# Queries of batch 2 loaded earlier and transposed by the DMA crossbar, with the units round its memory sums in a new order

## The chip, the cores and the metric

The kernel runs on one core of a Trainium2 chip. Five engines work side by side, each through its own list of instructions in order: TensorE (PE, with its weight loads as PEld) multiplies, VectorE (DVE) and ScalarE (ACT) work elementwise and read TensorE's results out of PSUM, GpSimd (POOL) works elementwise on SBUF, and SyncE (SP) only issues transfers. POOL, SP and ACT issue transfers to 16 DMA engines that they share. An instruction that must wait holds everything behind it on its engine. The metric is the device time of one execution in microseconds (us).

## The reference

There are 8 batches of 8 heads, 576 tokens and 64 dimensions, and 32 memory slots a head. Tokens are pooled into the slots by softmax weights; each query attends to its head's 32 pooled slots; the result, 4608 tokens of 512 features, goes through a gated feed-forward block with 1536 inner features.

```python
a = np.exp(phi - phi.max(2)); a = a / a.sum(2)     # per head: 576 x 32
k_m, v_m = a.T @ k, a.T @ v                        # memory sums: 32 x 64
scores = (q @ k_m.T) / 8                           # 576 x 32
x = softmax(scores) @ v_m                          # heads side by side: 4608 x 512
out = (silu(x @ w_gate) * (x @ w_val)) @ w_out     # 512 -> 1536 -> 512
```

## The kernel before

Matrix products take bf16 inputs. A batch goes through these steps.

- *Loads.* POOL issues most of them: `load_k`, `load_v` and `load_q` (L97 to L110) convert float32 to bf16 on the way. Weights come in three blocks of 512 inner features: gate and value (`load_w`), then w_out (`load_wo`, which fills `WO`). POOL's loads land in the order of their issue. The program is written so that an issue waits for the landing of the eighth load before it, as the same completion counter is used again.
- *Memory sums.* `phi_exp` (L170) takes exponentials on ACT. `kv_items` (L292) returns two units: `run_sums` multiplies phi with k and v on TensorE (L230) and then, on VectorE, takes the reciprocal of the denominators (L262) and scales the sums (`kv_norm`, L268, recorded as L266); `kv_T` (L278) transposes the scaled sums on TensorE (L288) and copies them to SBUF as `kT` (L289).
- *Queries.* They are needed transposed, as `qT`. Batches 0 to 2 use `q_T` (L377): TensorE transposes 18 blocks of 128x128 against the identity, six to a PSUM bank, and VectorE or ACT copies each bank out (L337, L339). Batches 3 to 7 use `load_qT` (L114): SP issues one transfer that transposes through the DMA crossbar, SBUF to SBUF, once the queries have landed.
- *Scores and softmax.* `scores` (L392) multiplies `kT` with `qT` on TensorE and ACT takes the exponential.
- *Gated block.* The value sums are multiplied into the gate and value weights (`u_round`, giving U); then gate and value products, silu on ACT and the product with the values on VectorE give `h`.
- *Output.* w_out is applied by a fast multiplication with seven products for eight. `weight_sums(c)` builds four sums of w_out's block c on VectorE, the matrices `T`; POOL or VectorE builds the same kind of sums of `h`, called `S`. `products(b, ...)` (L689) returns for a batch its seven products of six units each in a flat list; a unit is two matmuls, 0.109 us each by the profile's chain. Units 0 to 5 gather in bank "s", 6 to 11 in bank "a", 12 to 17 in "c", 18 to 23 in "s" again; units 4 and 5 of a product use w_out's block 2, units 2 and 3 block 1. After a product, `keep` (L748) copies a bank out on ACT (p1, q6, p5) or `add` (L757) adds banks on VectorE into an output tile, which SP stores.

The order of all this is written out by hand: the program runs with a manual schedule, so each engine's list is the order of the calls. Two stages matter here.

The opening issues the loads of batches 0 and 1, then (L905 to L916) the gate and value weights, w_out block 0, k of batch 2, w_out block 1, phi of batch 2, w_out block 2, v of batch 2. Further loads are hung on steps of the gated block by `beside_sums` (L672): when the first block of batch 0 is done, phi of batch 3 and the queries of batch 2; later queries, k and v of batch 3.

After the gated block of batches 0 and 1 the loop starts with batch 2 (L997 to L1022). Its lists are `zero` and `one`, the output units of batches 0 and 1, `kv`, the two units of the memory sums of batch 2, and `q2`, the three units of its query transposes, all copied out by ACT. TensorE runs units 0 to 5 of `zero`, 6 to 11 of `zero`, 0 to 5 of `one`, the sums, two query units, eight units of `zero` that read T and S of blocks 0 and 1, `kv_T`, the last query unit, four units of `zero` that read T of block 2, and then the scores of batch 2. VectorE builds T of blocks 0 and 1, scales the sums, builds the first half of T of block 2, copies `kT`, and builds the second half; POOL waits for that half (`wait_for`, L645) before it builds two blocks of S for batch 1.

Of the kernel before, what the change touches and what calls it, by code (L numbers as in the profile page):

```python
# [14 lines left out]
def kernel(  # L15
# [19 lines left out]
    nc = tc.nc  # L35
# [39 lines left out]
    def bank(shape, dtype, name):  # L75
        tag = free.pop(0)
        t = ps.tile(shape, dtype, tag=tag, name=name)
        held[id(t)] = tag, t
        return t

    def done(*tiles):

        for t in tiles:
            free.append(held.pop(id(t))[0])
# [3 lines left out]
    def head_pairs(x):  # L88

        return x.rearrange("h s d -> (h s d)").rearrange("(i p f) -> p i f", i=NP, p=128)  # L90

    def load_phi(b, eng):
        t = inp.tile([128, NP, JK * M], FP32, tag="phi", name="t_phi")
        eng.dma_start(out=t, in_=head_pairs(phi[b]))
        phis[b] = t
# [9 lines left out]
    def load_q(b):  # L105

        t = inp.tile([128, NS * 128], BF16, tag=f"q{Q_SLOT[b]}", bufs=1, name="t_q")
        nc.gpsimd.dma_start(  # L108
            out=t,
            in_=q[b].rearrange("h s d -> (h s d)").rearrange("(p f) -> p f", p=128),  # L110
        )
        qs[b] = t

    def load_qT(b):  # L114

        qTs[b] = att.tile([128, NS, 128], BF16, tag="qT", name="t_qT")
        nc.sync.dma_start_transpose(out=qTs[b], in_=qs[b])
# [10 lines left out]
    def load_w(which, c, half=None):  # L128

        src = (moe_w_gate, moe_w_val)[which]  # L130
        split = half is not None
        if not half:
            W[which, c] = wpool.tile(
                [128, 2, NP, HC] if split else [128, NP, CH], BF16,
                tag=f"W{which}{c}", name=f"W{which}{c}",
            )
        f0, n = (half * HC, HC) if split else (0, CH)
        nc.gpsimd.dma_start(  # L138
            out=W[which, c][:, half] if split else W[which, c],
            in_=src[:, c * CH + f0:c * CH + f0 + n].rearrange("(i p) f -> p i f", p=128),  # L140
        )
# [9 lines left out]
    def load_wo(c):  # L151
        t = wpool.tile([128, 4, DM], BF16, tag=f"WO{c}", name=f"WO{c}")
        nc.gpsimd.dma_start(
            out=t,
            in_=moe_w_out[c * CH:(c + 1) * CH, :].rearrange("(i p) f -> p i f", p=128),
        )
        for i in range(4):
            WO[4 * c + i] = t[:, i]
        WOc[c] = t
# [8 lines left out]
    ephis, rSs, bkvs, kTs, es, atts = {}, {}, {}, {}, {}, {}  # L168
# [91 lines left out]
    def kv_reciprocal(b, p):  # L260
        r = att.tile([128, NG], FP32, tag="rS", name="t_rS")
        nc.vector.reciprocal(out=r, in_=p)  # L262
        rSs[b] = r
# [14 lines left out]
    def kv_T(b):  # L278


        kTs[b] = att.tile([128, 3, 128], BF16, tag="kT", name="t_kT")
        t = bkvs.pop(b)
        if b > 3:
            nc.sync.dma_start_transpose(out=kTs[b], in_=t.rearrange("p n x -> p (n x)"))
            return
        p = bank([128, 3, 128], BF16, "p_T")
        for n in (2, 0, 1):
            nc.tensor.transpose(p[:, n], t[:, n], ident)  # L288
        nc.vector.tensor_copy(out=kTs[b], in_=p)  # L289
        done(p)  # L290

    def kv_items(b, beside=None):  # L292


        def run_sums():
            o = 2 * D
            behind = b in esums
            own = beside and not behind
            if own:
                d = bank([128, NG], FP32, "p_S")  # L300
                kv_denominators(b, d)
                kv_reciprocal(b, d)
                done(d)
            p = [bank([128, CH], FP32, f"p_kv{g}") for g in range(NG)]
            if not (own or behind):
                kv_denominators(b, p[0][:, o:o + NG])
            kv_sum(b, p, (0, 1))
            if behind:
                beside()
                kv_denominators(b, p[0][:, o:o + NG])  # L310
            if not own:
                kv_reciprocal(b, p[0][:, o:o + NG])
            kv_norm(b, p)
            if beside and not behind:
                beside()

        return [run_sums, lambda: kv_T(b)]
# [17 lines left out]
    def copy(eng, out, in_):  # L335
        if eng == "a":
            nc.scalar.copy(out=out, in_=in_)  # L337
        else:
            nc.vector.tensor_copy(out=out, in_=in_)  # L339
# [307 lines left out]
    def quad_sums(qd):  # L647
# [22 lines left out]
                    subtract(nc.gpsimd, t[:, 2], A12, t[:, 1])  # L670

    beside_sums = {  # L672
        (0, 0): lambda: (load_phi(3, nc.gpsimd), load_q(2)),
        (1, 0): lambda: load_q(3),
        (0, 1): lambda: (load_k(3), load_v(3)),
    }
# [152 lines left out]
    def q_items(b, evac):  # L829
        return [lambda n=n: q_T(b, n, evac[n]) for n in range(3)]  # L830
# [14 lines left out]
    def u_values(b):  # L845

        u_round(b, (((1,), 1, (0, 1)),), "aa")
    def run(items):
        for x in items:
            x()  # L850
# [13 lines left out]
    def gv_slots(b):  # L864
        return [lambda s=s: gv_slot(b, s) for s in range(2 * NJF)]
# [42 lines left out]
    for c in range(1, NCH):  # L908
        for which in range(2):
            load_w(which, c)  # L910
    load_wo(0)
    load_k(2)
    load_wo(1)
# [35 lines left out]
    warm(8)  # L949


    g0, g1 = gv_slots(0), gv_slots(1)
    nc.scalar.preload_act_table_set("silu_and_others")
    run([u_half(0, (0,), 0, 0, "va")])
# [41 lines left out]
    for b in range(2, B):  # L996
        last = b + 1 == B  # L997
        exp_tables()
        if b == 2:
            load_qT(3)  # L1000
            phi_exp(2)
            (zero, ops0), (one, ops1) = products(0, ("c11",)), products(1, ("p1", "c11"))
            kv, q2 = kv_items(2), q_items(2, "aaa")
            run(zero[:6])
            sums = {n: f for n, f in zip(((1, 1), (0, 2), (1, 2)), late)}
            late.clear()
            sums[0, 2]()
            weight_sums(0)
            weight_sums(1)
            run(zero[6:12] + one[:6] + kv[:1] + q2[:2])  # L1010
            weight_sums(2, (0, 1))
            run(zero[12:16] + zero[18:22] + kv[1:] + q2[2:] + zero[16:18] + zero[22:24])
            weight_sums(2, (2, 3))
            ops0["c11"]()
            ops1["p1"]()
            wait_for(Ts[2][0:1, 3, 0, 0:1])
            for part in ((0, 1), (3,), (2,)):
                for c in (1, 2):
                    sums[1, c](part)
            loads(4)  # L1020
            backlog = one[6:12] + zero[36:] + one[12:36]
            ops = ops1  # L1022
        else:
            run(take(6))
        for g in range(NG):
            scores(b, g)
        if b > 2:
            ops["p1"]()
            u_values(b)
        else:  # L1030
            run(zero[24:36] + take(6))
        run(take(6))
        z_inv_v(b, 0)
        ops["c11"]()
        run(take(6))
        if not last:
            phi_exp(b + 1)
        z_inv_v(b, 1)
        if b > 2:
            norm(b, 0)  # L1040
            norm(b, 1)
        run(take(6))
        run_late()
        if b == 4:
            wait_for(atts[4, 1][0:1, 0, 0:1])
            quad_sums(0)
        nc.scalar.preload_act_table_set("silu_and_others")
        run(take(6))
        if b == 2:
            norm(2, 0)  # L1050
        run(take(6))
        if b == 2:
            norm(2, 1)
            u_three(2)
            run(one[36:])
        g = gv_slots(b)
        quad = []
        if b == 4:
            quad = products(b, (), 0)[0]
        if last:  # L1060
            rest, rest_ops = products(b, (), 1)
            backlog += rest[:12]
        beside = 0 if last else 2 if quad else min(4, len(backlog))
        outs = [lambda: run(take(1)) for _ in range(len(backlog) - beside)]
        streams = [(g, 0, 24), (quad[:12], 0, 3), (quad[12:], 12, 18.5)]
        streams += [(outs, 4, 7 if quad else 24)]
        if b == 2:
            streams += [([lambda: u_values(2)], 2.5, 3)]
        if last:
            streams += [([u_item(b, 2)], 5, 6)]  # L1070
        if not last:
            if b > 2:
                load_qT(b + 1)
            if b > 2 and b != 4:
                phi_sum(b + 1)
            streams += [
                (kv_items(b + 1, lambda: (u_item(b, 2, "aava")(), run(take(2)))), KV, KV + 4),
                ([lambda: (u_three(b + 1), run(take(2)))], 19, 20),
            ]
        spread(*streams)  # L1080
        flush_mul()
        units, ops = products(b, ("p1", "c11"))
        backlog += units
# [34 lines left out]
```

## Time and profile before

| what | us |
|---|---|
| three timed runs | 233.19, 233.52, 233.64 |
| median | 233.52 |
| span of the profiled execution | 231.4 |
| median less span: what lies around the span | 2.1 |
| TensorE busy in the span | 221.6 |
| VectorE busy | 185.1 |
| ScalarE busy | 171.7 |
| GpSimd busy | 140.8 |

The page gives the profiled execution's span, from its first instruction to its last, and no separate time for it; the difference to the median of the timed runs stands in the table as what lies around it. The mean granted TensorE clock is 0.997 of full speed. Matmuls overlap one another, so the busy time of TensorE is no measure of its peak; what an interval is worth is read from when the next instruction starts. A row of the chain gives start, duration and work; a row of a group or of the order in time gives the engine, the line, the operation, the tiles it writes and reads, and how many instructions it merges. In a row on windows the columns are the stretch, its length, busy time of PE, PEld, DVE, ACT and POOL with the number of instructions, the granted clock, the DMA engines' mean busy share (above 1 where transfers overlap on an engine) and GB/s. POOL's loads are all on one DMA queue, SP's transfers on another.

### The profile page before, as it was taken

How to read it: one execution, taken by the hardware profiler on the slowest of the kernel's cores; microseconds unless marked ns; L12 is line 12 of the kernel's file. 1: busy time of each engine (PE TensorE's matmuls, PEld its weight loads, DVE VectorE, ACT ScalarE, POOL GpSimd, SP SyncE). 2: the span in 40 equal slices, each digit the busy share in tenths (PEclk: the TensorE clock that was granted, in tenths of full speed). 3: DMA queues.
4: the chain of work that ended last, by engine and by line, in shares of the span. 5: the costliest groups of instructions: out<-in, count | busy, mean ns of one | idle time of the engine just before them, and what ended most of it. 6: DMA issues, size and time to landing. Idle time of an engine off the chain costs nothing.

```text
span 231.4 us, 7210 instructions
## 1 busy us (share of the span) xinstructions
PE 221.6 (96%) x2825; PEld 169.8 (73%) x2825; DVE 185.1 (80%) x423; ACT 171.7 (74%) x365; POOL 140.8 (61%) x190
## 2 busy tenths in 40 slices
PE   6987799999999999999999999999999999999993
PEld 2544476778887777878788787887788778878882
DVE  4245789999966799989997668998999899977732
ACT  2777898988447989968896658978898789677310
POOL 8422427998199049765977689464845394039291
PEclk9999999999999999999999999999999999999998
DMA  6999999999996992999299946994014502202125
GB/s 214 210 211 206 199 207 207 221 245 268 205 225 175 256 256 49 223 204 184 71 223 191 226 134 115 252 236 89 28 65 114 104 0 95 91 10 84 31 85 160
DMA packets 36674, 36.84 MB, mean 159 GB/s; under 512 B 14624, under 2 KB 31008, under 8 KB 36640
## 3 DMA queue, kind: packets, MB, share of 16 engines
q0 software_dynamic: 16272, 22.42, 52.5%
q1 hardware_dynamic: 19600, 13.18, 22.9%
q10 hardware_dynamic: 768, 0.79, 1.1%
q8 instruction: 22, 0.36, 0.6%
q14 instruction: 12, 0.10, 0.1%
HBM read 42.47 MB, written 9.44 MB: 224 GB/s over the span
## 4 chain that ended last, share of the span: by engine, by line
PE 86%; DMA 9%; POOL 2%; ACT 1%; issue 0%; DVE 0%; POOLq 0%
PE p_g L515 21%; PE p_os L727 21%; PE p_v L515 20%; PE p_oc L727 10%; DMA W<-in_moe_w_val_dram 9%; PE p_oa L727 5%; PE p_u L472 5%; PE p_kv L230 2%; PE p_g L396 1%; POOL t_kv L99 1%; POOL t_kv L103 1%; PE p_q L383 0%; POOL t_q L108 0%; ACT t_qT L337 0%; POOL W L138 0%
## 5 line engine op out<-in xcount | busy, mean ns | idle before, releaser
L538 DVE TENSOR_TENSOR t_h<-t_sg,p_v 128x288 bf16<-128x288 bf16 x192 | 81.8, 451 | 14.1 <-PE p_v L515 7.0
L515 PEld LDWEIGHTS <-t_U 128*128 128x128 bf16 x768 | 73.9, 98 | 21.2 <-issue 3.5
L532 ACT ACTIVATE t_sg<-p_g 128x288 bf16<-128x288 f32 x192 | 73.3, 424 | 17.1 <-PE p_g L515 11.4
L515 PE MATMUL p_g<-t_A,t_U 128*128 128x288 bf16 x384 | 77.0, 286 | 0.0
L515 PE MATMUL p_v<-t_A,t_U 128*128 128x288 bf16 x384 | 77.0, 286 | 0.0
L727 PEld LDWEIGHTS <-t_S 128*128 128x128 bf16 x384 | 37.5, 98 | 4.5 <-issue 0.2
L603 POOL TENSOR_TENSOR t_S<-t_h 128x512 bf16<-128x512 bf16 x17 | 19.7, 1157 | 32.7 <-DVE t_h L538 31.2
L727 PEld LDWEIGHTS <-t_h 128*128 128x128 bf16 x288 | 27.1, 98 | 8.6 <-issue 5.0
L492 ACT CAST t_U<-p_u 128x512 bf16<-128x512 f32 x51 | 27.0, 605 | 6.6 <-PE p_u L472 6.6
L727 PE MATMUL p_os<-t_T,t_S 128*128 128x256 bf16 x192 | 23.7, 273 | 0.0
L560 POOL TENSOR_TENSOR t_S<-t_S,t_h 128x512 bf16<-128x512 bf16 x17 | 19.6, 1156 | 1.3
L560 POOL TENSOR_TENSOR t_S<-t_h 128x512 bf16<-128x512 bf16 x16 | 18.4, 1152 | 0.0
L560 POOL TENSOR_TENSOR t_S<-t_h,t_S 128x512 bf16<-128x512 bf16 x16 | 18.4, 1152 | 0.0
L472 PE MATMUL p_u<-W,t_kT 64*32 64x512 bf16 (+1 forms) x416 | 15.3, 363 | 1.2 <-DMA W<-in_moe_w_gate_dram 0.6
L496 DVE CAST t_U<-p_u 128x512 bf16<-128x512 f32 x21 | 13.6, 683 | 1.9 <-PE p_u L472 1.9
L727 PE MATMUL p_os<-t_T,t_h 128*128 128x256 bf16 x96 | 14.8, 273 | 0.0
L875 PE MATMUL p_warm<-bones 128*128 128x512 bf16 x44 | 12.5, 421 | 1.7 <-DVE bones L897 1.7
L452 DVE TENSOR_TENSOR t_A<-t_E,t_lz 128x576 bf16<-128x576 bf16 x16 | 11.4, 740 | 0.7 <-ACT t_lz L428 0.7
L727 PE MATMUL p_oc<-t_T,t_S 128*128 128x256 bf16 x96 | 11.9, 273 | 0.0
L727 PE MATMUL p_oa<-WO,t_h 128*128 128x256 bf16 x96 | 11.8, 273 | 0.0
L727 PE MATMUL p_oc<-WO,t_S 128*128 128x256 bf16 x96 | 11.8, 272 | 0.1
L727 PE MATMUL p_os<-WO,t_h 128*128 128x256 bf16 x96 | 11.8, 273 | 0.0
(107 smaller groups left out, 308.3 us busy)
## 6 DMA issues: line engine op xcount, KB each, us to landing
out_dram<-t_o SPq DMA_DIRECT2D x11, 512.0 KB, 3.0
t_kv<-in_k_dram POOLq DMA_DIRECT2D x8, 576.0 KB, 10.5
t_q<-in_q_dram POOLq DMA_DIRECT2D x8, 576.0 KB, 8.4
t_kv<-in_v_dram POOLq DMA_DIRECT2D x8, 576.0 KB, 14.7
t_phi<-in_phi_dram POOLq DMA_DIRECT2D x6, 576.0 KB, 8.1
out_dram<-t_o SPq DMA_DIRECT2D x10, 256.0 KB, 4.5
WO<-in_moe_w_out_dram POOLq DMA_DIRECT2D x3, 512.0 KB, 19.2
W<-in_moe_w_gate_dram POOLq DMA_DIRECT2D x2, 512.0 KB, 16.5
```

The source lines that it names most:

```text
L230: nc.tensor.matmul(p[g][32 * i:32 * i + 32, 0:n], lhsT=phi_of(b, g, j, i), rhs=kvs[b][64 * g:64 * g + 64, w0:w1, i, j * D:(j + 1) * D], st ...
L452: nc.vector.tensor_tensor(out=a, in0=es.pop((b, g)), in1=lzs.pop((b, g)), op=ALU.mult)
L472: nc.tensor.matmul(p[g][32 * i:32 * i + 32, o:o + n], lhsT=kTs[b][64 * g:64 * g + 64, 2, 32 * i:32 * i + 32], rhs=w_part(w, c, i, g, halve ...
L492: nc.scalar.copy(out=t, in_=p)
L496: nc.vector.tensor_copy(out=t, in_=p)
L515: nc.tensor.matmul(p[:, 0:HALF], lhsT=Us[b, c, g][:, o // 2, which, 128 * (o % 2):128 * (o % 2 + 1)], rhs=atts[b, g][:, r], start=(g == 0) ...
L532: nc.scalar.activation(out=sg, in_=gate[:, 0:HALF], func=AF.Silu)
L538: nc.vector.tensor_tensor(out=dst, in0=sg, in1=val[:, 0:HALF], op=ALU.mult)
L560: eng.tensor_tensor(out=out, in0=x, in1=y, op=ALU.subtract)
L603: eng.tensor_tensor(out=t[:, 0], in0=A21, in1=A22, op=ALU.add)
L727: nc.tensor.matmul(mine[home][:, u], lhsT=lhs(c, m, u), rhs=rhs(c, m), start=fresh and u == 0, stop=(k == 5), skip_group_check=u == 1 or n ...
L875: nc.tensor.matmul(p[:, 0:128 * a], lhsT=bones, rhs=x.to_broadcast([128, a, 128]) if a > 1 else bones, start=True, stop=True,)
```

## The change

Four things are done together. The queries of batch 2 are loaded directly behind the gate and value weights, ahead of w_out's blocks, and no longer beside the load of phi of batch 3. SP transposes them through the crossbar; the transfer stands first in SP's list behind the load of phi of batch 0, ahead of the transpose of batch 3's queries. The three query units leave the loop's start, with 18 TensorE transposes and three ACT copies. The remaining units are put in a new order: eight units of `zero` that read blocks 0 and 1 now run ahead of the memory sums, pairwise in turns from banks "c" and "s", four units that read block 2 run between the sums and `kv_T`, and the scores follow `kv_T` directly. On VectorE the first half of T of block 2 now stands ahead of the scaling of the sums. The copy of `kT` of batch 2 moves from VectorE to ACT, where it stands behind the copies p5 and q6.

```diff
@@ kv_T
-        nc.vector.tensor_copy(out=kTs[b], in_=p)
+        copy("a" if b == 2 else "v", kTs[b], p)
         done(p)
...
@@ beside_sums
-        (0, 0): lambda: (load_phi(3, nc.gpsimd), load_q(2)),
+        (0, 0): lambda: load_phi(3, nc.gpsimd),
...
@@ opening loads
     for c in range(1, NCH):
         for which in range(2):
             load_w(which, c)
+    load_q(2)
     load_wo(0)
     load_k(2)
     load_wo(1)
...
@@ before the gated block of batches 0 and 1
+    load_qT(2)
     g0, g1 = gv_slots(0), gv_slots(1)
...
@@ the loop, b == 2
-            kv, q2 = kv_items(2), q_items(2, "aaa")
+            kv = kv_items(2)
             run(zero[:6])
...
             weight_sums(0)
             weight_sums(1)
-            run(zero[6:12] + one[:6] + kv[:1] + q2[:2])
             weight_sums(2, (0, 1))
-            run(zero[12:16] + zero[18:22] + kv[1:] + q2[2:] + zero[16:18] + zero[22:24])
+            run(zero[6:12] + one[:6] + zero[12:14] + zero[18:20] + zero[14:16] + zero[20:22])
+            run(kv[:1] + zero[16:18] + zero[22:24] + kv[1:])
             weight_sums(2, (2, 3))
             ops0["c11"]()
             ops1["p1"]()
```

## The prediction

> **What bounds the kernel now.** I read the page's engine rows and slices first, then the chain of waits around the changed place, then the order in time of each engine there, and last the DMA queues: what each transfer moves and when it lands.
>
> ```profile
> PE 221.6 (96%) x2825; PEld 169.8 (73%) x2825; DVE 185.1 (80%) x423; ACT 171.7 (74%) x365; POOL 140.8 (61%) x190
> PE   6987799999999999999999999999999999999993
> DMA  6999999999996992999299946994014502202125
> ```
>
> TensorE is busy 96% of 231.4 us, and its slices are full from 27 us on. The third line matters as much: the DMA engines are full from the start to about 69 us (twelve slices of 5.8 us). So in the first third every transfer that is added makes each later one land later, while after 70 us there is room.
>
> ```profile
> 55.63 1.31 PE p_oa L727 x12
> 56.94 1.31 PE p_os L727 x12
> 58.25 0.20 PE p_kv L258 x9
> 58.46 0.73 PE p_kv L230 x72
> 59.19 0.78 PE p_q L383 x12
> 59.97 0.87 PE p_oc L727 x8
> 60.84 0.87 PE p_os L727 x8
> 61.71 0.17 PE p_T L288 x3
> 61.88 0.35 PE p_q L383 x6
> 62.23 0.02 issue
> 62.25 0.80 ACT t_qT L337
> 63.05 0.50 ACT t_p L752
> 63.55 0.04 issue
> 63.59 0.49 PE p_oc L727 x3
> ```
>
> This is the chain through the changed place. TensorE has no gap from 54 to 62 us: what is taken out there is worth its full price, and what is put in as a wait costs its full price. At 62.25 the chain goes through ScalarE: its last copy of transposed queries, then its copy of p5 (L752), which the units at 63.59 need because they write the same bank.
>
> ```profile
> WO<-in_moe_w_out_dram POOLq DMA_DIRECT2D x1, 512.0 KB, 19.2
> ...
> t_qT<-t_q SPq DMA_TRANSPOSE x1, 8.7
> ...
> 61.40:65.30 3.90, 3.84 (x52) 3.17 (x51) 2.24 (x7) 3.05 (x8) 2.22 (x3) 1.00 1.21 208
> 65.40:67.40 2.00, 2.00 (x20) 1.80 (x19) 1.45 (x3) 0.34 (x2) 1.92 (x3) 1.00 1.28 140
> 67.40:68.60 1.20, 1.20 (x13) 1.08 (x11) 1.13 (x3) 0.00 (x0) 1.20 (x2) 1.00 1.28 289
> ```
>
> The first two are single DMA issues (KB where given, us from issue to landing). The third block of w_out was issued at 32.21 and lands at 32.21 + 19.2 = 51.4; in the same way v of batch 2, issued at 34.76, lands 19.5 later, at 54.3. The second is the crossbar transpose of batch 3's queries, issued at 61.43. The last three are windows, GB/s at the end of each line: loads alone (208), the loads' end beside the crossbar transpose of batch 3's queries (140), that transpose alone (289).
>
> **What is removed.** 18 query transposes leave TensorE: 0.78 + 0.35 = 1.13 us by the chain's rows. Three copies of 0.80 us leave ScalarE. With them goes the wait at 63.59: from the first score (63.10) to the next unit TensorE takes 0.49 us, where the same scores in batch 3 take 92.74 - 92.48 = 0.26. The p5 copy will be over by then, so 0.23 us more goes. Removed: 1.36 us.
>
> **What the new order exposes.** Before, kv_T (the transposes of the memory sums) was followed by six query transposes and four units, 0.35 + 0.87 = 1.22 us that hid the copy of kT. Now nothing lies between kv_T and the scores. From 54.16 on, in order: zero[:6], zero[6:12], one[:6] to 58.09; eight of the new units, 1.75 us (the rows of 0.87 twice), to 59.84; the memory sums as before, 1.03 (58.09 to 59.12), to 60.87, the last result at 60.94; four units, 0.87, to 61.74. VectorE needs after the sums 0.04 + 0.16 (reciprocal) + 0.03 + 0.99 (the four scalings, one row) = 1.22, so kv_T starts at 62.2, not 61.74. Its three transposes are through 0.33 later and the copy starts 0.04 after that, as it did on VectorE (61.88 to 61.92), at 62.57. On ScalarE the copy of 384 columns is not shown; its copies of 256 and 768 columns take 0.372 and 0.799, which bound it; by their line it takes 0.48. ScalarE's p5 and q6 copies are over by 62.55. The scores start at about 63.07. Before they started at 63.10: the 1.13 us is given back as waiting. Against the next unit's 63.59 the balance is -0.03 - 0.23, about -0.25 us. The bounds: if VectorE and ScalarE hid all of it, -1.36; if the copy took 0.80 and each hand-over 0.1 more, +0.3. I take -0.25, since every term has a near row.
>
> The units moved forward read the halves of T on VectorE. Of block 1, the second matrix of T ends at 59.38 (58.96 + 0.42) and its units start at 59.40; a wait of 0.1 there is within the error. Block 1 is done at 60.06 (59.64 + 0.42), block 2's first half 0.8 later at 60.9, which pushes nothing: the sums end at 60.94, and the units that read it start at 60.87.
>
> **What the moved load costs.** load_q(2) goes from behind phi of batch 3 to before the three blocks of w_out. Query loads landed 2.5 and 2.8 us after the one before them (56.1, 58.6, 61.4). With 2.8, to be safe, the third block lands at 54.2 (2.5 would make it 53.9). TensorE takes it up as the ninth of zero[:6]'s twelve matmuls: 54.16 + 8 x 0.109 = 55.03. Alone, the load leaves 0.8 us of its 3.6 us of slack.
>
> **What the crossbar transpose costs.** It is new work in the full stretch, not moved work. SP waits only for q of batch 2, which takes the place of w_out's first block, right behind the last value weights (24.11 + 15.5 = 39.6): it lands at about 42.3. In batch 3 the first transpose packets flowed 4 us after issue (61.43 to 65.4); so here at 46.3, while block 2 of w_out is on its way, with block 3 still behind. Engine time that it takes from the loads, called X:
> - low end: 589,824 bytes at 289 GB/s, all by itself, 2.0 us. Nearer nothing if it fills gaps only; the busy share of 1.2 leaves none to see, but I keep 0 as the outermost end.
> - high end: in 65.40 to 67.40 the loads moved 0.09 MB, against 0.40 MB in an undisturbed 2.0 us (62.4 to 64.4): 1.55 us lost for 0.19 MB of transpose, for 0.59 MB 4.8 us. The loads were running out there, so this is too high.
> - taken: 2.9 us, nearer the low end for that reason.
>
> So block 3 lands at 54.2 + 2.9 = 57.1, and TensorE stands 57.1 - 55.03 = 2.1 us in the middle of zero[:6]. X = 0 gives no stall, X = 4.8 one of 4.0.
>
> [...]
>
> **What is hidden.** Memory of batch 2: v lands at 54.3 + 2.8 + 2.9 = 60.0; the sums start at 59.84 + 2.1 = 61.9. phi lands at 49.1 + 5.7 = 54.8, its exponential began at 55.59; a miss of 1 us would still be over before TensorE needs the bank behind it. POOL: its issues wait for the landing of the eighth load before (idle 1.67 us until the first k landed, ahead of the third weight issue). So v goes out when a gate block lands (21.29 + 15.8 = 37.1) and not at 34.76, and the sums queued behind it start 1.1 us later; 0.55 us of this comes back where load_q(2) stood (42.70); POOL then has 6.17 us of idle time. SP is idle from 1.2 to 61.43, so the new transpose delays nothing there; but queries of batch 3 land about X later (the load ahead of them has only moved), so their transpose and the stores behind it go out about 2.9 us later. The first store of o1 landed at 67.48 + 4.5 = 72.0, 2.9 later is 74.9; VectorE's c22 of batch 1 needs its buffer at 74.30, now 76.2: covered by about 1 us.
>
> **Sum.** -0.25 + 2.1 = +1.9 us. TensorE has 0.09 us of gaps from 63.1 to 76.4 and its slices are full to the end, so nothing takes it up. The profile gives a span of 231.4; the timed runs have a median of 233.52, 2.1 above it, which I take as what lies around the span. 231.4 + 1.9 + 2.1 = 235.4.
>
> **The rivals.**
> - *The DMA work hides (X up to 1.0).* For it: 3.6 us of slack; a fuller mix of two queues. Against: a DMA row at nine tenths or more in every slice there. The stall is at most 0.2: 233.3, no change to tell.
> - *The chain from sums to scores is hidden too: faster.* One mechanism: VectorE and ScalarE hand over kT inside the four units' 0.87 us, and block 3 is in time. The waits must shrink from 1.16 us to under 0.9 and X stay under 1. At best 233.5 - 1.36 = 232.2. Against: VectorE's 1.22 us is one dependent string of rows.
> - *The two queues take turns packet by packet.* Then each of an engine's 144 transpose packets (2304 of 256 bytes over 16) waits behind a load packet, 0.089 us by the undisturbed 2.0 us (361 packets, 16 engines), and takes 0.014 itself (2.0 us alone): 14.8 us, from 46.3 to 61.1, still ahead of the scores at 63.1. By the time block 3 lands, some 95 of them are through, X is 1.3, the stall 0.5: 233.8, not to be told from no change. Against: in 65.40 to 67.40, 734 transpose packets went beside 88 load packets, so it isn't turn for turn, and batch 3's queries landed 8.7 us after issue, here 51.0.
>
> [...] The row of 8.7 us for 18 blocks says 0.48 us each.
>
> **How the numbers follow.** The block-3 stall as forecast: 0.67; hidden: 0.13; faster: 0.12; turn for turn: 0.08. Changes under 0.2% (0.47 us) can't be told from none for this kernel. The stall gives more than that from X = 1.5 on, which I put at 0.65 of its 0.67, and turn for turn might by its errors, 0.03. Slower: 0.68. Same: 0.13 + 0.02 + 0.05 = 0.20. Faster: 0.12. The range holds the hidden case at its low end, 233.25, with 0.25 for the hand-overs' errors; at its high end X = 4.8, 231.4 + 2.1 - 0.25 + 4.0 = 237.3, with half of the 1 us that a late store or phi can add. The faster case lies outside. The stall's own range is 234.0 to 237.3.
>
> **What will show it.** TensorE with a gap of about 2 us near 55 us, released by the DMA of w_out; that block landing near 57; the transpose issued near 42 and landed by 54; scores of batch 2 near 65; before them a gap of 0.4 us at kv_T and one of 0.7 at the scores, released by VectorE and ScalarE. Wrong would be: no gap at 55 us, since then X is under 1 and the sum is -0.25; or a store or phi coming late, which adds up to 1 us.

## The result and the profile after

| what | before | after |
|---|---|---|
| median, us | 233.38 | 241.31 |
| lowest and highest | 233.19 to 233.64 | 239.33 to 242.85 |
| ratio, 95% interval | | 1.0337 [1.0312, 1.0362] |
| span of the profiled execution | 231.4 | 239.5 |
| time of that execution | | 241.34 |

The change costs 7.9 us. The forecast was 235.4 with a range from 233.0 to 237.8: the sign is right, the size is four times the forecast of 1.9, and the time lies outside the range.

The page of the kernel after, its engine row and slices (each slice is 6.0 us here, not 5.8):

```profile
PE 222.4 (93%) x2807; PEld 169.6 (71%) x2807; DVE 185.1 (77%) x422; ACT 170.1 (71%) x363; POOL 140.6 (59%) x190
PE   7977899996849999999999999999999999999992
PEclk9999999999979999999999999999999999999999
DMA  6999999999999996299459984998021702202124
```

TensorE's row was full from the sixth slice to the last but one; now the tenth is a 6 (54 to 60 us), the eleventh an 8 and the twelfth a 4 (66 to 72 us). In the twelfth the granted clock is 0.7 of full speed, which it was nowhere in the kernel before. VectorE is as busy as before, 185.1 us. The rest of the kernel runs as before, only later: the first gate product of batch 2 starts at 83.75 where it started at 76.35, the last matmul at 234.74 where it started at 227.33. So 7.40 us are lost before 83.75 and none behind it; the other 0.7 of the two spans' difference lies behind the last matmul, in the end of the last stores, and was not followed.

The chain of waits of the kernel after, in order of time:

```profile
42.21 0.19 PE p_v L515 x2
42.40 26.50 DMA t_qT<-t_q
68.89 0.04 issue
68.94 0.28 PE p_g L396
...
69.38 2.58 PE p_oc L727 x12
71.95 1.81 PE p_os L727 x12
73.77 1.31 PE p_oa L727 x12
```

Before, this stretch of the chain was TensorE throughout, with ScalarE's copies from 62.25 to 63.55. Now one transfer holds it for 26.50 us: the crossbar transpose, issued at 42.40 and landed at 68.9. Two groups of twelve matmuls behind it take 2.58 and 1.81 us where the third, equal group takes 1.31.

TensorE in order of time in the kernel after (start, us, then the work and in brackets the wait before it):

```profile
54.15 1.04 PE L727 MATMUL p_os<-WO,t_h 128*128 128x256 bf16 x8
57.58 0.60 PE L727 MATMUL p_os<-WO,t_h 128*128 128x256 bf16 x4 [2.39 <-DMA WO<-in_moe_w_out_dram]
...
65.00 0.34 PE L288 MATMUL p_T<-ident,t_bkv 128*128 128x128 bf16 x3 [0.32 <-DVE t_bkv L266]
68.94 0.28 PE L396 MATMUL p_g<-t_qT,t_kT 64*32 64x288 bf16 x1 [3.60 <-DMA t_qT<-t_q]
```

The first wait is the one that was forecast, nearly where and as long as forecast: block 3 of w_out at 57.5. The second was not forecast. In the runs below in which the scores wait for `kT` alone, they start 0.91 us behind the transposes of the memory sums (62.33 to 63.24 in the first of them), so here they could have started at 65.91; the transposed queries cost 68.94 - 65.91 = 3.03.

Windows of the kernel after: the wait, and the units behind it (columns as before; the granted clock is the third number from the end).

```profile
66.00:68.90 2.90, 0.00 (x0) 0.00 (x0) 0.20 (x1) 0.58 (x1) 2.82 (x3) 1.00 1.35 148
69.30:73.60 4.30, 4.30 (x32) 3.23 (x25) 0.69 (x1) 1.32 (x4) 4.24 (x4) 0.60 1.28 164
```

Here is the third piece. TensorE starts nothing in the first window (its wait is 3.60 in all), and behind it its clock is 0.60 for 4.3 us. By the chain this costs 2.58 + 1.81 - 2 x 1.31 = 1.77 us. The pieces make 65.91 - 63.10 = 2.8 to where the scores could have started, 3.0 of waiting for transposed queries, 1.8 of halved clock, less 0.2 for the wait that no longer stands behind the scores (0.49 us from the first score to the next unit and 1.47 for the twelve units there, against 0.44 and, at full clock, 1.31): 7.4.

Why 26.5 us? The DMA queues of the kernel after, 48 to 49 us, while the transpose is on its way (queue, packets, MB, share of the 16 engines' time; q0 is POOL's loads, q1 is SP's):

```profile
DMA packets 302, 0.19 MB, mean 194 GB/s; under 512 B 150, under 2 KB 302, under 8 KB 302
q0 software_dynamic: 152, 0.16, 91.2%
q1 hardware_dynamic: 150, 0.04, 29.1%
```

One transpose packet went here for one load packet, 150 beside 152. That is turn for turn, the rival that the prediction gave 0.08. A transpose packet holds 256 bytes, a load packet here some 1000, so SP's queue got 0.04 of 0.19 MB. At 150 packets a us the 2304 packets would need 15 us; from the first, near 46.4, to the landing it took 22.5: the pace went with that of the load packets, as the table shows. Counted from the trace's packets in stretches of 2 us:

| us | load packets | of these with 4608 bytes | transpose packets |
|---|---|---|---|
| 48 to 50 | 289 | 38 | 285 |
| 58 to 60 | 248 | 53 | 248 |
| 60 to 62 | 123 | 91 | 121 |
| 62 to 64 | 105 | 70 | 111 |
| 66 to 68 | 138 | 16 | 111 |

Turn for turn to 64 us, and half as many where most loads come in rows of 4608 bytes, which take 0.18 to 0.36 us each against 0.1 for one of 1024 bytes. From 66 to 68 there are few of both though the rows are short; why is not known.

### The profile page after: what moved, and what is told of

It reads as the page before. It is cut to its first block, busy times and chain, and to the rows that moved or that the text cites. A ratio compares the mean times of both kernels' runs of the same rounds, so it can differ in the third digit from the quotient of the medians.

```text
span 239.5 us, 7179 instructions
## 1 busy us (share of the span) xinstructions
PE 222.4 (93%) x2807; PEld 169.6 (71%) x2807; DVE 185.1 (77%) x422; ACT 170.1 (71%) x363; POOL 140.6 (59%) x190
## 4 chain that ended last, share of the span: by engine, by line
PE 76%; DMA 19%; POOL 2%; issue 0%; DVE 0%; POOLq 0%
PE p_os L727 19%; PE p_g L515 18%; PE p_v L515 17%; DMA t_qT<-t_q 11%; PE p_oc L727 10%; DMA W<-in_moe_w_val_dram 8%; PE p_u L472 5%; PE p_oa L727 5%; PE p_kv L230 2%; PE p_g L396 1%; POOL t_kv L99 1%; POOL t_kv L103 1%; POOL t_q L108 0%; POOL W L138 0%; DVE t_q L339 0%
## 5 line engine op out<-in xcount | busy, mean ns | idle before, releaser
L727 PEld LDWEIGHTS <-t_S 128*128 128x128 bf16 x384 | 38.3, 100 | 5.4 <-issue 0.2
L727 PE MATMUL p_os<-t_T,t_S 128*128 128x256 bf16 x192 | 24.4, 277 | 0.0
L727 PE MATMUL p_os<-t_T,t_h 128*128 128x256 bf16 x96 | 14.8, 273 | 0.0
L727 PE MATMUL p_oc<-WO,t_S 128*128 128x256 bf16 x96 | 13.0, 290 | 0.0
```

The costliest lines, as they stand in the source:

```text
L727: nc.tensor.matmul(mine[home][:, u], lhsT=lhs(c, m, u), rhs=rhs(c, m), start=fresh and u == 0, stop=(k == 5), skip_group_check=u == 1 or n ...
```

## The experiments

In the kernels that set `qTs[2] = qTs[1]`, and in those built on them, batch 2's attention reads batch 1's transposed queries in place of its own. That takes the wait for the transpose away and leaves the work as it is.

### The new order without the transfers

```diff
-    load_q(2)
...
-    load_qT(2)
+    qTs[2] = qTs[1]
```

> The changed kernel without the early load and without the crossbar transpose of batch 2's queries; the scores of batch 2 read the transposed queries of batch 1, so batch 2's attention is left out of the computation. What stays is the new order of the units, kT copied by ScalarE, and 18 transposes fewer on TensorE. Theory (the loss is all in the transfers): TensorE has no gap near 55 us, the scores of batch 2 start near 63.1 after two short waits of 0.4 and 0.7 us, and the time is 0.25 us under the kernel before, 233.1. Rival (the new order costs more than forecast): scores later than 64, time over 234.

Measured: 233.22, ratio 0.9979 [0.9961, 0.9997]. Its TensorE:

```profile
62.33 0.34 PE L288 MATMUL p_T<-ident,t_bkv 128*128 128x128 bf16 x3 [0.32 <-DVE t_bkv L266]
63.24 0.29 PE L396 MATMUL p_g<-t_qT,t_kT 64*32 64x288 bf16 x1 [0.57 <-ACT t_kT L337]
```

The scores start at 63.24, forecast 63.07, and the next unit 0.37 us later, not 0.26. The transposes that TensorE no longer does come back as waits for the sums and for `kT`, and what is left is a gain of 0.17 in the medians where -0.25 was forecast (in the traces the unit behind the scores starts at 63.61 here and at 63.59 before). So a version of this change whose transfers cost nothing at all would win 0.2% at most.

### The early load alone

The kernel after with the early load, but no transpose:

```diff
-    load_qT(2)
+    qTs[2] = qTs[1]
```

> The same with the early load put back, still no crossbar transpose (the loaded queries are read by nobody, batch 2's attention is left out). Theory: block 3 of w_out lands 2.8 us later than before, at 54.2, just ahead of its use at 55.0; no stall, time 233.1 as without the load. Rival (the load alone makes block 3 late): a gap near 55 us, and the time over 234.

Measured: 233.53, ratio 1.0002 [0.9990, 1.0015]. The twelve units at 54.30 run through without a gap:

```profile
54.30 1.47 PE L727 MATMUL p_os<-WO,t_h 128*128 128x256 bf16 x12
...
59.43 0.60 PE L727 MATMUL p_oc<-t_T,t_S 128*128 128x256 bf16 x4 [0.16 <-DVE t_T L560]
```

With the load the new order loses its gain, 0.3 us against the run before: part of it is the wait at 59.43 for VectorE's sums of block 1, which the prediction had put within its error.

### The early load in the kernel before

The same from the other side: the kernel before, with TensorE's transposes and its order, and only `load_q(2)` moved.

```diff
-        (0, 0): lambda: (load_phi(3, nc.gpsimd), load_q(2)),
+        (0, 0): lambda: load_phi(3, nc.gpsimd),
...
+    load_q(2)
     load_wo(0)
```

> The kernel before with one part of the change: the load of batch 2's queries goes ahead of w_out's blocks; they are still transposed on TensorE. Theory (the load alone fits into block 3's slack): block 3 lands near 54, no stall, time as before, 233.4 within 0.4. Rival (the earlier load makes something late): over 234.

Measured: 233.56, ratio 0.9995 [0.9980, 1.0009]. Neither the order nor the load, nor both together, makes the kernel slower. What is left is the transpose.

### The transpose, unread

Early load and transpose as in the kernel after, but nobody reads the result, and batch 3's transpose is written behind the scores.

```diff
     load_qT(2)
+    qTs[2] = qTs[1]
...
-            load_qT(3)
...
         for g in range(NG):
             scores(b, g)
+        if b == 2:
+            load_qT(3)
```

> The changed kernel with its early load and its crossbar transpose, but the scores of batch 2 read the transposed queries of batch 1 and so don't wait for the transpose (batch 2's attention is left out); the transpose of batch 3 is issued in a slightly later place. Theory (two separate losses: block 3 late by 2.4 us, then the wait for the transposed queries with the halved clock behind it): the gap of 2.4 us near 55 us stays, the wait before the scores and the half clock at 70 to 73 us vanish, time 233.5 + 2.4 - 0.25 = 235.6. Rival (the transfers' contention slows everything, whoever waits): still over 239.

Measured: 238.60, ratio 1.0218 [1.0189, 1.0246], 3 us above what the theory expected. The scores wait for `kT` alone, as expected, yet TensorE is 4.88 us late at the first gate product of batch 2. Its TensorE, and windows over it:

```profile
57.98 1.01 PE L727 MATMUL p_os<-WO,t_h 128*128 128x256 bf16 x4 [2.92 <-DMA WO<-in_moe_w_out_dram]
58.79 2.60 PE L727 MATMUL p_oa<-WO,t_h 128*128 128x256 bf16 x12
61.22 1.47 PE L727 MATMUL p_os<-WO,t_h 128*128 128x256 bf16 x12
```

```profile
58.90:59.90 1.00, 1.00 (x7) 0.69 (x6) 0.97 (x3) 0.59 (x1) 0.00 (x0) 0.50 1.20 257
...
60.90:61.90 1.00, 1.00 (x11) 0.86 (x9) 0.21 (x1) 0.00 (x0) 0.00 (x0) 0.91 1.16 241
```

Here block 3 came 0.4 us later than in the kernel after, and the clock halved behind this wait already (0.50 from 57.9 to 60.9 us). So this wait cost more than its length: the twelve matmuls at 58.79 take 2.60 us, the next twelve 1.47. I took the halved clock for the missing 3 us; the runs below with the fill and with the stores moved show that this was only part of it.

### Keeping TensorE busy before the scores

The kernel after, with 16 matmuls of 512 columns on constants, whose result nobody reads, ahead of the scores of batch 2.

```diff
             run(kv[:1] + zero[16:18] + zero[22:24] + kv[1:])
+            warm(64)
```

> The changed kernel with 16 matmuls of 512 columns on constants (about 3.4 us) put between the transposes of the memory sums and the scores of batch 2, where TensorE stands idle. Theory (the idle time makes the clock drop to half, which costs 1.8 us in the 24 matmuls behind the scores): granted clock 1.0 from 69 to 73 us, those 24 matmuls take 2.6 us instead of 4.4, and the time falls by 1.8 against the changed kernel's, to 239.5. Rival (the low clock has nothing to do with the gap): clock still 0.5 there, time unchanged at 241.3.

Measured: 241.35, ratio 1.0329 [1.0301, 1.0357]: no gain. In its trace block 3 was waited for 2.76 us and the clock halved there (twelve matmuls behind it take 2.70 us, the next twelve 1.47), so the fill came late and ran past the landing of the queries. It neither shows nor refutes the price of the clock.

### Keeping TensorE busy at both places

The same, and 11 such matmuls ahead of the units that need block 3.

```diff
-            run(zero[:6])
+            run(zero[:4])
+            warm(44)
+            run(zero[4:6])
```

> The changed kernel with both places where TensorE stands idle filled with matmuls on constants: 11 of 512 columns (2.4 us) ahead of the units that need block 3 of w_out, 16 (3.4 us) ahead of the scores of batch 2. The first fill was missing in the run with one fill, where the clock halved behind the stall of 2.8 us on block 3 and slowed the second fill itself. Theory (an idle time of about 2.5 us and more halves the clock for some 3 us): clock 1.0 throughout from 55 to 75 us, and the time 1.8 us under the changed kernel's 241.3, 239.5. Rival (the low clock has another cause): half clock still there, no gain.

Measured: 240.44, ratio 1.0299 [1.0262, 1.0337]. Windows of this run over the whole stretch, two of five:

```profile
58.00:62.00 4.00, 4.00 (x39) 3.60 (x37) 3.05 (x9) 0.58 (x1) 0.00 (x0) 1.00 1.17 254
...
70.00:75.00 5.00, 5.00 (x54) 4.49 (x47) 2.81 (x5) 1.30 (x4) 4.92 (x6) 1.00 1.27 163
```

The clock is full in every window, and TensorE is 6.40 us late at batch 2's first gate product, not 7.40 (the trace is what tells this; the two kernels' times overlap at their ends). So here the halved clock came of TensorE's idleness (1.00 with the fills, 0.60 for 4.3 us behind the wait without), and full clock gives about 1 us back, not the 1.8 of the chain: the queries landed at 68.8, and the second fill overran that by 0.8 (scores at 69.61), since with the clock full the memory sums ahead of it reach v of batch 2 before it has landed, which the halved clock had hidden in the run before:

```profile
63.66 0.80 PE L230 MATMUL p_kv<-t_kv,t_ephi 64*32 64x128 bf16 x72 [0.73 <-DMA t_kv<-in_v_dram]
```

### Empty queue for the transpose

The loads of q, phi, k and v of batch 3 are held until VectorE's reciprocal for the sums of batch 2, near 64 us, so that POOL's queue runs empty while the transpose is on its way.

```diff
-        (0, 0): lambda: load_phi(3, nc.gpsimd),
-        (1, 0): lambda: load_q(3),
-        (0, 1): lambda: (load_k(3), load_v(3)),
...
-            load_qT(3)
...
             run(kv[:1] + zero[16:18] + zero[22:24] + kv[1:])
+            wait_for(rSs[2][0:1, 0:1])
+            load_q(3)
+            load_phi(3, nc.gpsimd)
+            load_k(3)
+            load_v(3)
+            load_qT(3)
```

> The changed kernel with the four loads of batch 3 (queries, phi, k, v) held back on POOL until VectorE has taken the reciprocal of batch 2's sums, near 63 us, so that behind v of batch 2 (landed at 62.8) POOL's queue is empty; the transpose of batch 3's queries follows its load. Theory (the transpose takes turns with the loads packet by packet, 150 to 150 in one us): from 59 on it no longer meets the long rows of queries and phi, and its 2304 packets are through near 63; it lands by 64, the scores don't wait for it, and the time falls by the 3.6 us of that wait and the 1.8 of the half clock behind it, to about 236; 1.5 more if the clock halves behind the stall on block 3. Rival (the transpose is slow by itself once it is issued amid loads, whatever follows): it lands at 68 to 69 as before, time 241.

Measured: 249.12, ratio 1.0656 [1.0616, 1.0697]. The queues from 59 to 60 us, when the loads run out, and then the transpose as an issue, with its time to landing:

```profile
q1 hardware_dynamic: 453, 0.12, 82.6%
q0 software_dynamic: 76, 0.07, 43.7%
```

```profile
t_qT<-t_q SPq DMA_TRANSPOSE x1, 19.2
```

As the load queue empties, the transpose's pace triples (453 against 150 packets a us), and it lands 19.2 us after its issue instead of 26.5. The scores then wait for `kT` only, at 65.77, and from 55 to 76 us the clock is 1.00 in every window. So here the neighbours in the other queue set the landing. The time was missed altogether, for another reason: on SP, batch 3's transpose now stood waiting for its late queries, with the stores of batches 0 and 1 behind it. VectorE's and SP's rows:

```profile
DVE t_o L754 <- DMA out_dram<-t_o: 10.8, 1, 10.8
```

```profile
42.44 35.67 SPq L117 DMA_TRANSPOSE t_qT<-t_q  x2
78.17 14.54 SPq L680 DMA_DIRECT2D out_dram<-t_o  x8
```

The first store goes out at 78.17, VectorE's addition lacks a free output tile for 10.8 us, and TensorE lacks the bank that the addition empties.

### Held loads, with the stores ahead

The same with `load_qT(3)` behind the stores of batches 0 and 1.

```diff
-            load_qT(3)
...
+        if b == 2:
+            load_qT(3)
         g = gv_slots(b)
```

> The loads of queries, phi, k and v of batch 3 held until the sums of batch 2, as in the run with held loads, but the transpose of batch 3's queries stands on SP behind the stores of batches 0 and 1. Theory: the 10.8 us of that run came from stores behind the transpose on SP; with the stores ahead the wait of VectorE's output addition is gone. The transposed queries of batch 2 land near 61.6 as there and the scores do not wait; the stall for block 3 stays at 2.4 and the clock behind it at 1. If the transpose of batch 3, issued near 78 us, lands before its scores (92.5 in the kernel before, about 95 here), the time is 235.5 to 236.5. Rival: it meets the loads of batch 4 and takes turns with them, lands 15 to 20 us after issue, and holds the scores of batch 3 up to 3 us, with a halved clock behind: 237 to 241.

Measured: 241.42, ratio 1.0339 [1.0298, 1.0380]: the rival's case, and 7.7 us better than the run before, so those stores had cost that much. The scores of batch 2 no longer wait for queries; those of batch 3 do, and VectorE's addition still waits, as the stores beside the held loads take 7.7 us (median of eight) to land. The waits, and batch 3's transpose from issue to landing:

```profile
PE p_g L396 <- DMA t_qT<-t_q: 1.6, 1, 1.6
...
PE p_os L724 <- DVE t_o L754: 1.5, 1, 1.5
```

```profile
t_qT<-t_q SPq DMA_TRANSPOSE x1, 16.0
```

Issued at 82.15, it meets the loads of batch 4 and lands 16.0 us later; in the kernel before the same transfer took 8.7 us, where the loads ahead of it had run out. Its landing went with what else was under way.

### The load still earlier

If the landing at 68.9 is the trouble, issue it sooner: the load ahead of the last gate and value weights.

```diff
     for c in range(1, NCH):
         for which in range(2):
             load_w(which, c)
+        if c == 1:
+            load_q(2)
-    load_q(2)
```

> The changed kernel with the load of batch 2's queries one step earlier, ahead of the gate and value weights of block 3 of the inner features and not behind them. It lands near 37 and not 42.4, so its transpose starts 5 us sooner. Theory (turn for turn, about 22 us of packets): it lands near 63.5 and no longer holds the scores; block 3 of w_out is as late as before (stall 2.4 to 3 us), and the time is 235.6 to 237.5 by whether the clock halves. Rival (the weights behind the load come late too): a new gap on TensorE at 43 to 49 us, time 238 and more.

Measured: 241.06, ratio 1.0319 [1.0293, 1.0344]. The transpose is issued at 37.48 and lands 22.1 later, at 59.6, ahead of the scores. But now all of it goes ahead of block 3:

```profile
59.90 1.01 PE L727 MATMUL p_os<-WO,t_h 128*128 128x256 bf16 x4 [4.52 <-DMA WO<-in_moe_w_out_dram]
60.70 2.77 PE L727 MATMUL p_oa<-WO,t_h 128*128 128x256 bf16 x12
63.26 2.65 PE L727 MATMUL p_os<-WO,t_h 128*128 128x256 bf16 x12
```

The wait of 3.0 us at the scores is gone, that for block 3 has grown by 2.1, and the halved clock has moved from 69 us to 59 and got longer (0.50 from 59 to 65 us). The forecast of 235.6 to 237.5 was missed. The traffic of the transpose was paid here by the reader that came next.

### The unread transpose at full clock

Back to the 3 us that the unread run lost beyond the forecast: its kernel, with the fill ahead of block 3's units.

```diff
-            run(zero[:6])
+            run(zero[:4])
+            warm(44)
+            run(zero[4:6])
```

> The kernel with the transposed queries of batch 2 unread (attention of batch 2 reads batch 1's, so the output differs) and the transpose of batch 3 issued behind batch 2's scores, with 11 fill matmuls ahead of the two units that need block 3 of w_out. Theory: the 3 us above the forecast in the unread run came from the halved clock behind the wait for block 3 (2.60 us for twelve matmuls in place of 1.31, then 1.47); the fill keeps the clock full, the block lands when it did (about 57.8), and only the wait is left. Unread run 238.6 less 1.3 to 1.5 of halved clock: about 237.2, with no window between 57 and 62 us under a clock of 0.9. What then still stands above the kernel before, about 3.4, is the landing of block 3 (57.8 against 55.0, 2.8 us) and 0.6 that neither names. Rival: the halved clock costs nothing because something later absorbs it; then 238.6 again.

Measured: 238.49, ratio 1.0208 [1.0190, 1.0225]: no change, as the rival had it, though the clock is 1.00 in every window from 54 to 69 us. The scores start at 66.26, 1.3 us earlier than in the unread run, but TensorE is 4.95 late again at batch 2's first gate product. What took it back stands in the waits, and in SP's list:

```profile
PE p_os L727 <- DVE t_o L757: 1.9, 1, 1.9
...
DVE t_o L757 <- DMA out_dram<-t_o: 1.8, 1, 1.8
```

```profile
42.42 31.72 SPq L117 DMA_TRANSPOSE t_qT<-t_q  x2
74.19 31.19 SPq L683 DMA_DIRECT2D out_dram<-t_o  x9
```

The stores again. Queries of batch 3 land at 68.1, not 61.4, since the transpose of batch 2 has pushed every load behind it; SP issues their transpose at 68.9, which keeps it busy for 5.2 us, and only then the first store: 74.19 (74.14 in the kernel after) against 67.48 before.

### Stores ahead of batch 3's transpose, with and without the fill

Two kernels: the unread one with `load_qT(3)` behind the first four stores, with the fill at block 3 and without it.

```diff
-        if b == 2:
-            load_qT(3)
...
+        if b == 2:
+            load_qT(3)
         nc.scalar.preload_act_table_set("silu_and_others")
```

> The unread run with fill at block 3, but with the transpose of batch 3's queries behind the first four stores on SP (attention of batch 2 reads batch 1's queries, so the output differs). Theory: in the two unread runs a third bound takes over, the stores: queries of batch 3 land some 6 us later, SP's list holds the stores behind their transpose (first store at 74.19 against 67.48), VectorE's output addition waits 1.81 for its buffer and TensorE 1.93 for that. With four stores ahead this wait is gone: TensorE, 3.05 behind the kernel before at the third product of batch 0 (69.26 against 66.21), stays 3.05 behind, and the time is 233.5 + 3.1 = 236.6, if the stores land within 8 us beside the loads. Rival: something else takes the 1.9 back, and it stays at 238.5.

> The same without the fill. Theory: the halved clock behind the wait for block 3 costs 1.3 us (67.96 against 66.63 at the first products behind the scores), and it shows in the time now that the stores no longer hold TensorE: 236.6 + 1.3 = 237.9. Rival: the halved clock is taken back later whatever the order of the stores, and the two runs have the same time. (Where block 3 happens to wait under 2.5 us and the clock stays full, as in the changed kernel itself, both have the same time too: the trace tells.)

| unread transpose, us | clock halved behind block 3 | clock kept by fill |
|---|---|---|
| stores behind batch 3's transpose | 238.60 | 238.49 |
| four stores ahead of it | 238.28, ratio 1.0202 [1.0177, 1.0227] | 237.47, ratio 1.0167 [1.0145, 1.0190] |

Each alone gives 0.1 to 0.3 us, less than these runs can tell from nothing, as their times overlap; both together give 1.1, and the times of the two lower runs do not overlap (237.25 to 237.68, 237.83 to 239.05). By the waits, two limits lie side by side, and either holds when the other is gone. TensorE's waits in the run with both:

```profile
PE p_kv L230 <- DMA t_kv<-in_v_dram: 0.7, 1, 0.7
PE p_g L396 <- ACT t_kT L337: 0.6, 1, 0.6
PE p_T L288 <- DVE t_bkv L266: 0.3, 1, 0.3
PE p_os L727 <- DMA WO<-in_moe_w_out_dram: 0.3, 1, 0.3
```

No wait for stores is left. The 3.75 us that TensorE is still late at batch 2's first gate product are two loads: the units that need block 3 start at 58.03, 3.0 behind the 55.03 of the kernel before, and v of batch 2 adds 0.75. The theory's 236.6 lacked v and was 0.9 too low. In the run without the fill:

```profile
57.51 1.01 PE L727 MATMUL p_os<-WO,t_h 128*128 128x256 bf16 x4 [2.42 <-DMA WO<-in_moe_w_out_dram]
58.32 2.61 PE L727 MATMUL p_oa<-WO,t_h 128*128 128x256 bf16 x12
```

TensorE is 3.93 us late here, hardly more than with the fill, since in this execution the loads came sooner (block 3 at 57.5 and not 58.0, v at 62.6 and not 63.9): the fill's 0.8 us is the difference of the medians, the two traces show 0.2.

The clock halved here behind 2.42 us of waiting (0.50 from 57.5 to 60.5 us). In the kernel after and in both runs with held loads it stayed full behind 2.39, 2.42 and 2.41.

### Where the 7.9 us lie

| step | us | from |
|---|---|---|
| order and early load | about 0 | 233.22, 233.53, 233.56 |
| later landings of block 3 and v, all else made harmless | 4.0 | 237.47 less 233.50 |
| halved clock, and stores behind batch 3's transpose | 1.1 | 238.60 less 237.47 |
| the scores' wait for transposed queries, with the halved clock behind it | 2.7 | 241.31 less 238.60 |

The last two steps are known to about 0.6 us only: four runs of the kernel after went from 239.33 to 242.85.

## Why the prediction was wrong

*The expensive place was right.* That the load is harmless and the transpose's traffic is what counts ("What the moved load costs", "What the crossbar transpose costs") holds: two runs with the load alone show no change. Block 3 was forecast at 57.1 and landed at 57.5, its wait at 2.1 and was 2.4; how far this was luck stands below. The balance of "What the new order exposes" was -0.25; the run without transfers gave -0.17 (+0.02 by its trace). POOL's sums began 1.1 us later, as forecast.

*The step that failed is "What the crossbar transpose costs".* It priced the transpose only by what it takes from the loads, and put its own landing at 51.0, by the 8.7 us of batch 3's. That row is from a moment when the load queue was running out; here the queue was full throughout, and the landing was at 68.9. The window that the step used against the rival of turns, 734 packets beside 88, is the same moment: the load queue was running out there, and where it was full 150 went beside 152. So the likeliest case rested on a row from another state of the queue, while the rival that the packets bear out was given 0.08. The scores' wait for the transposed queries therefore had no term in the sum; it was 3.0 us, with a halved clock behind it. That rival's own sum was too short as well, 14.8 us: it took one size of load packet for all. Its landing of 61.1 was 7.8 us early and would have been harmless. It had the packets through by block 3's landing right (95 an engine; the trace has 1443 by 57.5, 90 an engine), but not what they take from the loads: 1.3 us there, 3.3 by the landing of block 3 (57.5, and 54.3 in the run with the load alone).

*X was mis-sized, and grows past block 3.* The 2.9 was the price of the whole transpose, between 2.0 and a 4.8 that was called too high. Where all of it went ahead of block 3, in the run with the load still earlier, block 3 landed at 59.9, which makes X 5.6. In the kernel after only 1443 of the 2304 packets had gone by 57.5; two errors met there, and the stall came out right partly by luck. X was taken once for all that follows. v was forecast at 60.0 and landed at 62.84, so X was 5.7 by then; queries of batch 3 were forecast 2.9 later and came 6.4 later. With that, "What is hidden" fails in two covers: v (hidden in the kernel after only because the scores are late anyway; 0.26 to 0.75 us in the runs with the first fill), and the stores, whose 1 us of cover against 2.9 is none against 6.7 (VectorE waited 1.8 where nothing else was later). In the kernel after the stores cost nothing, as TensorE is 7.4 us late by itself.

*The sum had no term for the clock.* The stall was priced at its length. Behind 3.60 us without a matmul the clock was 0.60 for 4.3 us, worth 1.8 by the chain; two pairs of runs show what it gives to keep TensorE busy, 0.9 and 0.8 us by the medians, 1.0 and 0.2 by the traces.

*No one figure a block fits the transpose.* The prediction read 0.48 us for each of the 18 blocks from the row of 8.7 us. In the kernel after the same transfer took 26.5 us, 1.47 us a block, and held the scores 3.0 us; among the landings in these runs are 8.7, 16.0, 19.2 and 26.5 us. In the window of the kernel before that has it alone, 289 GB/s flowed; beside loads, from 48 to 49 us in the kernel after, it moved 0.04 MB in the us, a fifth of what flowed.

*No placing tried here saves the change.* Earlier, the transpose holds block 3; later, the scores; with loads held, the stores or batch 3. Without any transfer the new order wins 0.17 us, so with this order of the units no placing of the transfers is likely to win more, and none of these kernels is worth keeping beside the one before.

## What to carry to other kernels

A landing time read from a trace belongs to the state of the other queues at that moment (8.7 to 26.5 us for the same transfer here): before moving a transfer of many small packets into a stretch where another queue is full, count its packets against the other queue's packets a us, and look at everything behind it in both queues, the stores too. And price a TensorE wait like those here, 2.4 to 4.5 us, at its length and up to a microsecond more, since half clock followed five of eight such waits; keeping TensorE busy gave 0.8 and 0.9 us by the medians. Removing the first wait here showed the next one just beneath.

## What the runs showed of the hardware

- *These two DMA queues shared the engines by packets, not by bytes.* From 48 to 49 us in the kernel after 152 load packets went beside 150 transpose packets, 0.16 and 0.04 MB. When the loads ran out, from 59 to 60 us in the run with loads held, the transpose had 453 packets in the us, beside 76 of loads.
- *TensorE's clock halved behind a wait of 2.42 us in one run, and not in another.* Waits of 2.42, 2.76, 2.92, 3.60 and 4.52 us were followed by half clock, waits of 2.39, 2.41 and 2.42 were not; why waits of one length ended differently was not shown. The stretches of half clock lasted 3.4 us in the kernel after (69.44 to 72.85) and in the run with four stores ahead and no fill, and 6.8 us (58.84 to 65.67) in the run with the load still earlier.
- *A transpose issue kept SP busy.* 10.4 us for batch 2's and 6.1 us for batch 3's in the kernel after; the first store on SP came behind both, at 74.14.
